# The last MLP's weight blocks: sums taken when the float64 weights are converted, second layer stored split, no GpSimd work in the last stage

## The chip, the cores and the metric

The kernel runs on one core of one Trainium2 chip, as one launch. The metric is device time in microseconds (us). Before the change it is 1503.79 us, the median of 3 runs (1501.11 to 1505.8). The core has five engines with a queue of instructions each: TensorE (PE in the profile; its weight loads are shown as PEld), VectorE (DVE), ScalarE (ACT), GpSimd (POOL) and SyncE (SP). Each works through its queue in order, and waits for another by semaphores. In this kernel SP issues all the large transfers.

## The reference, cut to what matters

An attention, a first MLP over tokens and channels, and then this block, whose last line but one is what the change is about:

```python
def _moe2_ref(x, w_ch1, w_ch2):          # x: 4 x 576 tokens x 512 channels
    X = np.fft.fft(np.fft.fft(x, axis=1), axis=2)
    u = x + np.real(X).astype(np.float32)
    mu = np.mean(u, axis=-1, keepdims=True)
    var = np.mean((u - mu) ** 2, axis=-1, keepdims=True)
    un = (u - mu) / np.sqrt(var + 1e-06)
    ch = np.maximum(un @ w_ch1, 0.0) @ w_ch2     # 512 -> 2048 -> 512
    return (u + ch).astype(np.float32)
```

All weights come as float64. [...]

## The kernel before

**Split products.** A float32 matrix `x` is kept as two parts in the fast matmul format: `hi`, a copy rounded to that format (one ACT instruction), and `lo = x - hi` (one subtraction on DVE or POOL). A product is three matmuls: hi·hi, hi·lo and lo·hi.

**Conversion** (`conv64`). A piece of 512 columns is loaded into a buffer `slot` (three of them), goes through one ACT and five DVE instructions and an addition on POOL (`cadd`), and is stored to DRAM. For the attention's and first MLP's weights (`parts` true) it is split on the way by `chi` (ACT) and `csub` (POOL), and both parts are stored. For the last MLP, 32 pieces of `wm2` are stored unsplit to `wd_d`: for each of 16 hidden blocks `f` of 128, 512 columns of the first layer's weights and 512 of the second's. The conversions run beside the attention.

**The last MLP** (`channel`) has two stages. The first 384 tokens go through plain products (`layer1`, `layer2`), f by f; `first_weights` loads 1024 columns of `wd_d` and splits them (`dwh` on ACT, `dwl` on DVE). The other 1920 tokens are the last stage: three tiles of 640 tokens (`p`), and for each eight pairs of hidden blocks (`q`), so 24 pairs (p, q). The first layer of a pair is a product of 2 x 2 blocks, done with seven block products in place of eight, which takes sums and differences of the blocks of both factors:

- `operands(p)` makes the seven parts of the tokens (`TH` on ACT, `TL` and the differences `TA` on DVE), once for each p.
- `factors(p, q)` makes the seven parts of the weights, for every pair anew, thus three times for each q: it loads the four raw blocks (`WR`, 512 KB, into `wraw`), splits the two that are used as they are (`WH` on ACT, `WL` on POOL), makes the four sums in place (`WA`, POOL), splits these (`WH`, `WL`), all into `wc` (two buffers), and loads and splits the second layer's weights (`VR`, 512 KB; `VH` on ACT, `VL` on POOL) into `v` (three buffers).
- `pair(p, q)` issues the seven products, `LP` (L1324), six matmuls of 320 columns each, and between them the steps that combine their results: `LE` on ACT (L1334) copies a bank of the accumulator out, `LC` on DVE (L1338) adds another bank to it. A pair needs four results, c11, c22, c21 and c12, and there are three banks: product 3 adds to a bank that the `LC` of c22 must have read. Then `hidden` makes the parts of the ReLU's result: `LH` on ACT (L1343) and `LL` on DVE (L1345), four of each, into `hp` (three buffers).
- `second(p, q)` issues 30 matmuls of 512 columns, `LQ` (L1383), into accumulators `y` and `c`. They run about three pairs behind the products.

So ACT's queue holds `LE`, `WH`, `LH` and `VH` in one line, and DVE's holds `LC` and `LL`.

**What sets the order.** Every step is an `Op` with an engine, a cost and a due time; `Plan.order` runs a list schedule over them and writes the instructions in that order into each engine's queue. `SHIFT` moves the due time of each kind of step. For the kinds named in `SHARED`, the planner adds time when DVE and POOL would work at once. At run time only the queues' order and the semaphores count.

Of the kernel before, what the change touches and what calls it, by code (L numbers as in the profile page):

```python
# [119 lines left out]

SHARED = ("cclamp", "cshift", "csign", "cexp", "cmul", "lo4", "FPUT", "dwl", "yadd", "ql.", "kl.", "q.", "un")


# [1434 lines left out]
```

## Time and profile before

| | us |
|---|---|
| median of 3 runs | 1503.79 |
| the profiled execution, its own time | 1502.83 |
| its span in the profile | 1501.0 |
| PE busy | 1433.9 (96%) |
| PEld busy | 1333.3 (89%) |
| DVE busy | 1048.3 (70%) |
| ACT busy | 760.3 (51%) |
| POOL busy | 860.0 (57%) |

The profiled execution's own time is its span and 1.8 us around it. Busy time of PE includes the modelled end of each matmul, so that it says when PE had work in flight and not that it ran at its rate. The first `LP` product starts at 1128.6 us after the span's start, the last one at 1473.5 us; behind them only `LQ` matmuls and the last additions are left.

### The profile page before, as it was taken

Reading aid. Unit: us, or ns where it says so; the run is one execution under the profiler, and the core shown is the slowest. Engines: PE = TensorE matmul, PEld = TensorE weight load, DVE = VectorE, ACT = ScalarE, POOL = GpSimd, SP = SyncE. Lnnn points to the kernel's source line nnn. Section 1 sums busy time; section 2 is a strip of 40 time slices with the busy share of each in tenths; the row PEclk is TensorE's granted clock in tenths of the full one; section 3 lists DMA queues with packets and bytes.
Section 4 is the critical chain, followed back from the end, with each engine's and each line's share of the span. In section 5 each row is a group of like instructions: output and inputs, shape, how many; then the busy total and the mean of one; then the engine's idle time right before and its main releaser. Section 6 shows DMA issues by size and latency. Waiting matters only on the chain.

```text
span 1501.0 us, 25069 instructions
## 1 busy us (share of the span) xinstructions
PE 1433.9 (96%) x9259; PEld 1333.3 (89%) x9259; DVE 1048.3 (70%) x1927; ACT 760.3 (51%) x1456; POOL 860.0 (57%) x653
## 2 busy tenths in 40 slices
PE   8999999999999999999999999999999998988988
PEld 6777789999999999999999999999988877878877
DVE  7867767878777788787787836757577665675452
ACT  4454577566556654665656545323354543443431
POOL 1444497787776675876677641102228885676651
PEclk8999999999999999999999999999999999999999
DMA  5887767856767676657785538762444222322211
GB/s 147 205 224 198 196 177 209 253 171 192 209 189 238 174 219 190 204 175 184 221 244 173 141 100 228 230 210 60 135 146 128 84 72 84 126 71 71 91 57 50
DMA packets 88661, 242.87 MB, mean 162 GB/s; under 512 B 9363, under 2 KB 18708, under 8 KB 88247
## 3 DMA queue, kind: packets, MB, share of 16 engines
q1 hardware_dynamic: 88538, 241.27, 54.8%
q8 instruction: 73, 1.20, 0.3%
q14 instruction: 50, 0.41, 0.1%
HBM read 164.94 MB, written 36.47 MB: 134 GB/s over the span
## 4 chain that ended last, share of the span: by engine, by line
PE 74%; DVE 8%; POOL 6%; DMA 4%; issue 3%; ACT 3%; SPq 2%; ACTq 0%; POOLq 0%; DVEq 0%
PE av L686 13%; PE bank L586 11%; PE bank L864 9%; PE bank L844 9%; PE s L665 9%; PE bank L1324 6%; DVE hp L1345 5%; PE y L1383 4%; DMA qq<-qx 3%; POOL wraw L1288 3%; POOL wc L1283 2%; PE bank L1174 2%; PE y L1196 2%; PE bank L807 2%; PE c L1020 2%
## 5 line engine op out<-in xcount | busy, mean ns | idle before, releaser
L678 POOL TENSOR_TENSOR pl<-s,ph 128x576 fp32r<-128x576 f32 x192 | 288.5, 1514 | 107.7 <-ACT ph L675 70.7
L592 DVE TENSOR_REDUCE mp<-bank 116x1 f32<-116x384 f32 x480 | 242.7, 551 | 87.9 <-PE bank L586 83.2
L670 ACT ACTIVATE s<-s 128x576 f32<-128x576 f32 (+1 forms) x320 | 189.6, 602 | 156.0 <-PE s L665 110.0
L586 PE MATMUL bank<-kk,qq 128*116 128x384 f32 x960 | 215.8, 349 | 15.3 <-DMA qq<-qx 7.4
L665 PE MATMUL s<-qq,kk 128*128 128x288 f32 (+1 forms) x1152 | 207.4, 303 | 0.6 <-ACT s L670 0.4
L675 ACT ACTIVATE ph<-s 128x576 fp32r<-128x576 f32 (+1 forms) x240 | 151.4, 634 | 106.1 <-PE av L686 104.7
L1324 PE MATMUL bank<-tt,wc 128*128 128x320 f32 x1008 | 168.3, 318 | 37.4 <-DVE e L1338 32.4
L1324 PEld LDWEIGHTS bank<-tt,wc 128*128 128x128 f32 x1008 | 156.6, 194 | 48.3 <-DVE e L1338 36.8
L586 PEld LDWEIGHTS bank<-kk,qq 128*116 128x116 f32 x960 | 161.7, 182 | 27.5 <-issue 10.1
L665 PEld LDWEIGHTS s<-qq,kk 128*128 128x128 f32 (+1 forms) x1152 | 177.8, 192 | 6.7 <-ACT s L670 1.4
L1283 POOL TENSOR_TENSOR wc<-wraw,wc 128x512 fp32r<-128x512 f32 (+2 forms) x72 | 111.0, 1557 | 115.3 <-ACT wc L1281 104.8
L844 PE MATMUL bank<-ut,w 128*128 128x320 f32 (+1 forms) x1152 | 176.2, 297 | 0.0
L1345 DVE SCALAR_TENSOR_TENSOR hp<-e,hp 128x320 fp32r<-128x320 f32 x96 | 115.4, 1248 | 69.5 <-ACT hp L1343 69.3
L864 PE MATMUL bank<-h,w 128*128 128x320 f32 (+1 forms) x1152 | 162.9, 296 | 0.1
L844 PEld LDWEIGHTS bank<-ut,w 128*128 128x128 f32 x1152 | 159.6, 190 | 0.0
L864 PEld LDWEIGHTS bank<-h,w 128*128 128x128 f32 x1152 | 156.4, 189 | 0.5 <-DVE h L768 0.4
L362 POOL TENSOR_TENSOR slot<-slot 128x512 f32<-128x512 f32 (+2 forms) x62 | 82.4, 1330 | 98.9 <-DVE slot L359 72.4
L686 PE MATMUL av<-pl,vh 128*65 128x288 f32 x432 | 127.0, 294 | 1.1 <-POOL pl L678 1.1
L686 PE MATMUL av<-ph,vh 128*65 128x288 f32 x432 | 127.7, 296 | 0.3 <-ACT xtr L691 0.3
L686 PE MATMUL av<-ph,vl 128*65 128x288 f32 x432 | 126.9, 294 | 0.0
L873 DVE TENSOR_TENSOR yt<-bank,yt 128x256 f32<-128x256 f32 (+1 forms) x192 | 85.7, 454 | 43.0 <-PE bank L864 40.7
L1383 PE MATMUL y<-v,hp 128*128 128x512 f32 x432 | 111.3, 396 | 0.0
(149 smaller groups left out, 2507.3 us busy)
## 6 DMA issues: line engine op xcount, KB each, us to landing
w<-wb_d SPq DMA_DIRECT2D x96, 512.0 KB, 4.3
slot<-in_wm_dram SPq DMA_DIRECT2D x56, 512.0 KB, 5.1
wraw<-wd_d SPq DMA_DIRECT2D x40, 512.0 KB, 3.8
kk<-kx SPq DMA_DIRECT2D x30, 576.0 KB, 5.0
wb_d<-slot SPq DMA_DIRECT2D x24, 512.0 KB, 3.7
vraw<-wd_d SPq DMA_DIRECT2D x24, 512.0 KB, 3.7
v<-in_v_dram SPq DMA_DIRECT2D x32, 292.5 KB, 4.2
qx<-in_qT_dram SPq DMA_DIRECT2D x15, 576.0 KB, 6.2
```

The lines of the kernel that those rows point to most:

```text
L586: nc.tensor.matmul(bank.t[:QM, :KW], qq.t[:r, t, q0:q0 + QM], kk.t[:r, t, c * KW:(c + 1) * KW], start=(t == 0), stop=(t == 1))
L592: tops.append(add("mr" + own_place, "V", t_dve(KW), dd, lambda bank=bank, j=j, c=c: nc.vector.tensor_reduce(out=mp.t[:QM, j, c:c + 1], in_ ...
L665: nc.tensor.matmul(ps.t[:, j, :HQ], kk.t[:r, t, (c0 + j) * 128:(c0 + j + 1) * 128], qq.t[:r, t, qs], start=(t == 0), stop=(t == 1))
L670: a = add(f"exp{own_place}{gr}", "A", t_act(n * HQ), due + 0.1, lambda ps=ps, s=s, n=n: nc.scalar.activation(out=s.t[:, :n], in_=ps.t[:, : ...
L675: h = add(f"hi{gr}", "A", t_act(n * HQ), due + 0.25, lambda ph=ph, s=s, n=n: nc.scalar.activation(out=ph.t[:, :n], in_=s.t[:, :n], func=AF ...
L678: a = add(f"lo{gr}", e, t(n * HQ), due + 0.4, lambda s=s, ph=ph, pl=pl, eng=eng, n=n: eng.tensor_tensor(out=pl.t[:, :n], in0=s.t[:, :n], i ...
L686: nc.tensor.matmul(po.t, vx.t[:, c0 + j], x.t[:, j], start=first and k == 0, stop=last and k == len(pairs) - 1)
L844: mms.append(lambda ps, k=len(mms), kk=kk, wi=wi, xi=xi, t0=t0, n=n: nc.tensor.matmul(ps[:, :n], view("p (s k n) -> p s k n", s=2, k=4)[:, ...
L864: mms.append(lambda ps, k=len(mms), x=x, wi=wi, hi=hi, cc=cc, t0=t0, n=n: nc.tensor.matmul(ps[:, :n], ww[x][2]("p (s n) -> p s n", s=2)[:, ...
L1324: nc.tensor.matmul(ps.t[:, :PH], w.t[:, wi, k, 128 * kk:128 * kk + 128], x.t[:, xi, kk], start=(first and m == 0), stop=(last and m == 5), ...
L1345: return [a, add("LL", "V", t_dve(PH), base(p, q) + SL * (slots[i] + 1) / 17, lambda: nc.vector.scalar_tensor_tensor(out=h.t[:, k, 1, cols ...
L1383: nc.tensor.matmul(y.t, h.t[:, k, hi, j * 128:(j + 1) * 128], v.t[:, wi, k], start=(q == 0 and k == 0 and n == 0), stop=(q == 7 and k == 1 ...
```

## The change

The four sums are made where the weights are converted, and stored beside the raw blocks, so that the last stage loads all seven (`w1_d`, 7 x 256 columns, 896 KB for a pair). `conv64` gets an argument `sums`: four POOL instructions of 128 columns in place (`cs`) behind `cadd`, and one more store. The host lays `wm2` out so that one piece of 512 columns holds one half of a pair's four blocks. The second layer's pieces are now split at the conversion (`parts` true) and stored as `w2_d` (1024 KB for a pair). In the last stage `WH` and `WL` become one instruction each of 1792 columns, `WL` on DVE; `WA`, `VH` and `VL` are gone; `VR` loads straight into `v`; and `wraw` has one buffer where there were two. In `first_weights` the second layer's half is loaded split (`dwv`), and `dwh` and `dwl` have 512 columns. Nearly every value of `SHIFT` is another one, and `SHARED` has four more kinds.

```diff
-    "cvld": 22.77, "cabs": 91.18, "cclamp": 306.7, "cshift": 206.5, "csign": 124.94, "cexp": 45.41, "cmul":
...
+    "cvld": 18.95, "cabs": 336.18, "cclamp": 653.39, "cshift": 93.62, "csign": 86.53, "cexp": 67.74, "cmul":
...
-SHARED = ("cclamp", "cshift", "csign", "cexp", "cmul", "lo4", "FPUT", "dwl", "yadd", "ql.", "kl.", "q.", "un")
+SHARED = ("TL", "TA", "LL", "WL", "cclamp", "cshift", "csign", "cexp", "cmul", "lo4", "FPUT", "dwl", "yadd", "ql.", "kl.", "q.", "un")
...
-    wd_d = dram.tile([F2, 128, 1024], F32, name="wd_d")
+    w1_d = dram.tile([F2 // 2, 128, 8, 2, 128], F32, name="w1_d")
+    w2_d = dram.tile([F2, 128, 2, 512], F32, name="w2_d")
...
+            if sums is not None:
+                done = a
+                for k, (x, y, op) in enumerate(((-4, -1, ALU.add), (0, -3, ALU.subtract), (-3, -4, ALU.subtract), (-2, 1, ALU.subtract))):
...
+                    done = add("cs", "P", t_pool(128), due, lambda k=k, x=x, y=y, op=op, quarter=quarter: nc.gpsimd.tensor_tensor(
+                        out=quarter(k), in0=quarter(x), in1=quarter(y), op=op), [done], uses=[w])
+                r.append(add("cvst", "SP", t_dma(512 * n), due, lambda: nc.sync.dma_start(
+                    out=sums, in_=f32(hi()).rearrange("p (s n) -> p s n", n=128)), [done], uses=[w]))
...
-        for f in range(F2):
-            for o in range(0, 1024, 512):
-                store((2, f), conv64(
-                    90.0 + f * 1.0, wm2[f][:, o:o + 512], [(wd_d[f][:, o:o + 512], same)], False))
+        for q in range(F2 // 2):
+            for k in range(2):
+                store((2, q), conv64(90.0 + 2 * q, wm2[q][:, 512 * k:512 * k + 512], [(w1_d[q][:, :4, k], blocks)], False, w1_d[q][:, 4:, k]))
+            for k in range(2):
+                store((3, 2 * q + k), conv64(
+                    91.0 + 2 * q, wm2[q][:, 1024 + 512 * k:1536 + 512 * k], [(w2_d[2 * q + k], same)], True))
...
-        vraw_r = late(1, "vraw", "mp", [128, 2, C])
+        wraw_r = late(1, "raw7", "mp", [128, 1792])
...
+                o = add("WR", "SP", t_dma(512 * 1792), d - 1.5, lambda: nc.sync.dma_start(
+                    out=raw.t.rearrange("p (i k n) -> p i k n", k=2, n=128), in_=w1_d[q][:, 1:]), ready, new=[raw])
...
-                w_ops = piece(0, 0, 512, 0, [o])
-                w_ops += piece(1, 768, 1024, 512, [o])
-                s1 = sums(0, 3, 2, 3, ALU.add, w_ops)
-                s3 = sums(1, 2, 0, 2, ALU.subtract, [s1])
-                s2 = sums(2, 0, 3, 0, ALU.subtract, [s3])
-                s4 = sums(3, 1, 1, 0, ALU.subtract, [s2])
-                w_ops += piece(5, 0, 1024, 768, [s4])
...
-                a = add("VH", "A", t_act(1024), d + 1.2, lambda: nc.scalar.activation(
-                    out=v.t[:, 0], in_=vraw.t, func=AF.Copy), [o] + late_w, new=[v], uses=[vraw])
...
+                a = add("WH", "A", t_act(1792), d, lambda: nc.scalar.activation(
+                    out=of(0), in_=raw.t, func=AF.Copy), [o], new=[w], uses=[raw])
+                b = add("WL", "V", t_dve(1792), d, lambda: nc.vector.tensor_tensor(
+                    out=of(1), in0=raw.t, in1=f32(of(0)), op=ALU.subtract), [a], uses=[raw, w])
+                o = add("VR", "SP", t_dma(512 * 2048), d, lambda: nc.sync.dma_start(
+                    out=f32(v.t), in_=w2_d[2 * q:2 * q + 2].rearrange("f p s n -> p s f n")), ready + late_w, new=[v])
+                return w, [a, b], v, [o]
```

On DVE, near the end of the program, this is the order for three pairs before (L1338 is `LC`, L1345 is `LL`):

```order
L1338 TENSOR_TENSOR e<-bank,e 128x320 x4
L1345 SCALAR_TENSOR_TENSOR hp<-e,hp 128x320 x4
L1338 TENSOR_TENSOR e<-bank,e 128x320 x4
L1345 SCALAR_TENSOR_TENSOR hp<-e,hp 128x320 x4
L1338 TENSOR_TENSOR e<-bank,e 128x320 x3
```

and now (L1337 is `LC`, L1344 is `LL`, L1301 is the new `WL`):

```order
L1337 TENSOR_TENSOR e<-bank,e 128x320 x4
L1301 TENSOR_TENSOR wc<-raw_16625,wc 128x1792
L1344 SCALAR_TENSOR_TENSOR hp<-e,hp 128x320 x4
L1337 TENSOR_TENSOR e<-bank,e 128x320 x4
L1344 SCALAR_TENSOR_TENSOR hp<-e,hp 128x320 x4
L1337 TENSOR_TENSOR e<-bank,e 128x320 x3
```

One long instruction came between a pair's additions and its `LL` block; the rest of the line is as it was. A group of four `LC` holds c22, c21 and c12 of one pair and c11 of the next.

On ACT at the same place, one pair before (L1334 is `LE`, L1281 `WH`, L1343 `LH`, L1303 `VH`):

```order
L1334 ACTIVATE e<-bank 128x320
L1281 ACTIVATE wc<-wraw 128x512
L1281 ACTIVATE wc<-wraw 128x256
L1334 ACTIVATE e<-bank 128x320 x2
L1281 ACTIVATE wc<-wraw 128x1024
L1343 ACTIVATE hp<-e 128x320 x4
```

and now (L1333 is `LE`, L1299 `WH`, L1342 `LH`):

```order
L1342 ACTIVATE hp<-e 128x320 x4
L1333 ACTIVATE e<-bank 128x320 x3
L1299 ACTIVATE wc<-raw_16625 128x1792
L1342 ACTIVATE hp<-e 128x320 x4
L1333 ACTIVATE e<-bank 128x320 x3
```

Before, the `WH` of 1024 columns, which splits the sums, stood in front of the four `LH`; now the one `WH` stands there.

On POOL, the last pairs before (L1283 is `WL`, L1288 `WA`, L1305 `VL`):

```order
L1283 TENSOR_TENSOR wc<-wraw,wc 128x1024
L1305 TENSOR_TENSOR v_16604<-vraw,v_16604 128x1024
L1283 TENSOR_TENSOR wc<-wraw,wc 128x512
L1283 TENSOR_TENSOR wc<-wraw,wc 128x256
L1288 TENSOR_TENSOR wraw<-wraw 128x256 x4
```

and now a piece near the end of the attention (L694 is the attention's `pl`, L363 `cadd`, L368 `csub`, L377 the new `cs`):

```order
L694 TENSOR_TENSOR pl<-s,ph 128x576 x2
L377 TENSOR_TENSOR slot<-slot 128x128
L694 TENSOR_TENSOR pl<-s,ph 128x576 x2
L363 TENSOR_TENSOR slot<-slot 128x512
L377 TENSOR_TENSOR slot<-slot 128x128
L694 TENSOR_TENSOR pl<-s,ph 128x576
L377 TENSOR_TENSOR slot<-slot 128x128
```

POOL's work for the last MLP now stands between the attention's instructions. Of the 64 `cs` and 16 new `csub`, 16 and 4 stand behind the attention's last `pl`, beside the Fourier transform, together with 7 `cadd`; the last instruction of POOL's queue is one of the transform's additions.

## Rows read from the trace of the kernel before

**Rows 1.** Stretches: us; busy (count) of PE, PEld, DVE, ACT, POOL; clock, DMA, GB/s.

```profile
40.00:865.00 825.00, 808.14 (x5552) 764.05 (x5551) 638.62 (x1228) 490.07 (x921) 551.30 (x399) 1.00 0.70 199
865.00:1043.30 178.30, 175.50 (x1318) 171.33 (x1317) 108.15 (x257) 64.30 (x141) 34.12 (x38) 1.00 0.57 174
1128.60:1473.80 345.20, 307.79 (x1671) 275.06 (x1670) 207.07 (x263) 147.89 (x288) 240.46 (x184) 0.98 0.26 85
```

**Rows 2.** Groups on PE by line, 1128.6 to 1473.8: busy, mean ns, idle before.

```profile
L1324 PE MATMUL bank<-tt,wc 128*128 128x320 f32 x1008 | 168.3, 318 | 37.4 <-DVE e L1338 32.4 <-ACT e L1334 5.0
L1383 PE MATMUL y<-v,hp 128*128 128x512 f32 x367 | 96.0, 397 | 0.0
L1383 PE MATMUL c<-v,hp 128*128 128x512 f32 x252 | 61.9, 390 | 0.0
L1139 PE MATMUL bank<-ident,un 128*128 128x128 f32 x40 | 5.7, 285 | 0.0
```

**Rows 3.** Chain that ended last, 1400 to 1501: start, us, what.

```profile
1432.42 3.51 PE bank L1324 x24
...
1438.54 4.92 DVE hp L1345 x3
...
1476.51 2.72 PE c L1383 x12
```

**Rows 4.** Timeline of one pair: start, us, engine, line, what, idle before it.

```profile
1423.57 5.66 DVE L1345 SCALAR_TENSOR_TENSOR hp<-e,hp 128x320 fp32r<-128x320 f32 x4 [4.65 <-ACT hp L1343]
...
1429.16 1.07 DVE L1338 TENSOR_TENSOR e<-bank,e 128x320 f32<-128x320 f32 x2
...
1429.69 2.03 PE L1324 MATMUL bank<-tt,wc 128*128 128x320 f32 x12 [1.71 <-DVE e L1338]
...
1432.25 3.67 PE L1324 MATMUL bank<-tt,wc 128*128 128x320 f32 x24
...
1436.88 1.06 ACT L1281 ACTIVATE wc<-wraw 128x1024 fp32r<-128x1024 f32 x1 [2.24 <-POOL wraw L1288]
...
1438.03 1.19 ACT L1343 ACTIVATE hp<-e 128x320 fp32r<-128x320 f32 x3
```

**Rows 5.** Lines L1345 and L1338: count, ns min/median/max.

```profile
L1345 DVE SCALAR_TENSOR_TENSOR hp<-e,hp x96: 469/814/2771, 1132.2 to 1478.3; 128x320 fp32r<-128x320 f32 x96
...
L1338 DVE TENSOR_TENSOR e<-bank,e x96: 465/492/494, 1131.1 to 1473.8; 128x320 f32<-128x320 f32 x96
```

**Rows 6.** Groups on POOL by line, 970 to 1501.

```profile
L1283 POOL TENSOR_TENSOR wc<-wraw,wc 128x512 fp32r<-128x512 f32 (+2 forms) x72 | 111.0, 1557 | 115.3 <-ACT wc L1281 104.8 <-PE y L1383 9.4 <-PE bank L1324 1.2
L1288 POOL TENSOR_TENSOR wraw<-wraw 128x256 f32<-128x256 f32 x96 | 82.8, 862 | 7.5
...
L1305 POOL TENSOR_TENSOR v<-vraw,v 128x1024 fp32r<-128x1024 f32 x24 | 60.6, 2527 | 23.1 <-ACT v L1303 23.1
```

**Rows 7.** Groups by form, whole span, that price the new instructions.

```profile
L367 POOL TENSOR_TENSOR slot<-slot 128x512 fp32r<-128x512 f32 x27 | 36.4, 1351 | 17.1 <-ACT slot L365 17.0
...
L1281 ACT ACTIVATE wc<-wraw 128x1024 fp32r<-128x1024 f32 x24 | 25.5, 1061 | 49.0 <-POOL wraw L1288 49.0
...
L1112 DVE TENSOR_TENSOR w<-wraw,w 128x1024 fp32r<-128x1024 f32 x16 | 19.5, 1218 | 9.8 <-ACT w L1110 9.7
```

**Rows 8.** SP's issues between 1286 and 1288, then the stretch of 1 us that ends them.

```profile
1286.41 0.36 SPq L1300 DMA_DIRECT2D vraw<-wd_d  x1
1286.82 0.46 SPq L1273 DMA_DIRECT2D wraw<-wd_d  x1
1287.33 0.46 SPq L1121 DMA_DIRECT2D u<-u_d  x1
...
1295.00:1296.00 1.00, 1.00 (x6) 0.83 (x5) 0.00 (x0) 0.82 (x1) 0.15 (x1) 1.00 0.14 45
```

**Rows 9.** Stretches of 10 us: the two of lowest clock in the stage.

```profile
1160.00:1170.00 10.00, 7.19 (x35) 6.41 (x34) 9.43 (x17) 6.49 (x16) 9.69 (x8) 0.83 0.17 54
...
1350.00:1360.00 10.00, 8.24 (x34) 7.69 (x35) 6.22 (x10) 3.25 (x6) 5.45 (x6) 0.66 0.23 73
```

More of the change, by code (lines that the diff above doesn't have):

```diff
@@ L76 @@
-    -220.37, "LP": -176.18, "LE": 274.63, "LC": -205.45, "LH": -55, "LL": 114.93, "LQ": 315.6,
+    "cvld": 18.95, "cabs": 336.18, "cclamp": 653.39, "cshift": 93.62, "csign": 86.53, "cexp": 67.74, "cmul":
+    24.33, "cadd": 136.67, "chi": 229.31, "csub": 137.36, "cvst": 12.38, "cs": 193.21, "warm.": -10.38, "l.":
+    -170.47, "q.": 3.29, "qh.": 173.09, "ql.": -56.56, "kh.": 73.63, "kl.": -86.48, "M.": -726.75, "mr.": 22.61,
+    "zh.": -56.2, "mr2.": -99.98, "zl.": -207.73, "mT.": 12.63, "mrow.": -142.63, "vld": -151.06, "S.": -27.39,
[6 rows of a table added]
@@ L77 @@
+    -401.58, "TH": 382.16, "TL": -581.56, "TA": -170.63, "WR": 111.46, "WH": -199.81, "WL": -528.64, "VR":
+    -831.72, "LP": -551.07, "LE": 609.89, "LC": -780.38, "LH": 25.74, "LL": 290.03, "LQ": 824.98,
 }
@@ L325, in tile_attention_moe_fnet, with conv64 @@
         converted = []
-        def conv64(due, src, outs, parts):
+        def conv64(due, src, outs, parts, sums=None):
             w = Buf(cvw)
@@ L1271, in factors @@
                 d = base(p, q) - 2.2
-                raw, w = Buf(craw_r), Buf(wc_r)
-                o = add("WR", "SP", t_dma(512 * 1024), d - 1.5, lambda: nc.sync.dma_start(
-                    out=raw.t.rearrange("p (f n) -> p f n", f=2),
-                    in_=wd_d[2 * q:2 * q + 2].rearrange("f p n -> p f n")[:, :, :C]), [more] + stores[2, 2 * q] + stores[2, 2 * q + 1], new=[raw])
+                raw, w, v = Buf(wraw_r), Buf(wc_r), Buf(v2_r)
+                ready = [more] + stores[2, q] + stores[3, 2 * q] + stores[3, 2 * q + 1]
@@ L1287, in sums @@
-                def sums(n, dst, x, y, op, deps):
-                    return add("WA", "P", t_pool(256), d + 0.3 + 0.05 * n, lambda: nc.gpsimd.tensor_tensor(
-                        out=raw.t[:, 256 * dst:256 * dst + 256], in0=raw.t[:, 256 * x:256 * x + 256],
-                        in1=raw.t[:, 256 * y:256 * y + 256], op=op), deps, uses=[raw])
-                w_ops = piece(0, 0, 512, 0, [o])
-                w_ops += piece(1, 768, 1024, 512, [o])
-                s1 = sums(0, 3, 2, 3, ALU.add, w_ops)
@@ L1295, in factors @@
-                s3 = sums(1, 2, 0, 2, ALU.subtract, [s1])
-                s2 = sums(2, 0, 3, 0, ALU.subtract, [s3])
-                s4 = sums(3, 1, 1, 0, ALU.subtract, [s2])
-                w_ops += piece(5, 0, 1024, 768, [s4])
-                vraw, v = Buf(vraw_r), Buf(v2_r)
-                o = add("VR", "SP", t_dma(512 * 1024), d, lambda: nc.sync.dma_start(
-                    out=vraw.t, in_=wd_d[2 * q:2 * q + 2].rearrange("f p n -> p f n")[:, :, C:]),
-                    [more] + stores[2, 2 * q] + stores[2, 2 * q + 1], new=[vraw])
@@ L1317, in product @@
                     x, x_ops = t[i]
[L1318 removed]
+                    k = {1: 0, 2: 1, 3: 6, 4: 2, 5: 3, 6: 4, 7: 5}[i]
                     def products():
@@ L1537 @@
     a_m1 = units(inputs["moe_w_ch1"], inputs["moe_w_ch2"], F1)
-    a_m2 = units(inputs["moe2_w_ch1"], inputs["moe2_w_ch2"], F2)
+    m = units(inputs["moe2_w_ch1"], inputs["moe2_w_ch2"], F2).reshape(F2 // 2, 2, 128, 8, 128)
+    a_m2 = _np.empty((F2 // 2, 128, 16, 128), m.dtype)
+    for k in range(2):
+        for n, (f, b) in enumerate(((1, k), (0, k), (0, 2 + k), (1, 2 + k))):
+            a_m2[:, :, 4 * k + n] = m[:, f, :, b]
+        a_m2[:, :, 8 + 4 * k:12 + 4 * k] = m[:, k, :, 4:]
+    a_m2 = a_m2.reshape(F2 // 2, 128, 2048)
     names = ["kT", "qT", "v", "wt1", "wt2", "wm1", "wm2", "cs", "ss", "cd", "sd", "nyq"]
```

42 lines of the change are left out of this document (18 added, 24 removed), and 12 rows, old and new, of the table SHIFT.

## Prediction

> **What bounds the kernel now.** I first read busy time by stretch. PE is busy 97.9% of the attention's stretch and 98.4% of the Fourier transform's, but 307.8 of 345.2 us where the seven-product scheme runs, which leaves 37.4 us idle there [rows 1]. Next I read who ended that idle time: all 37.4 us stand before `LP` (L1324), 32.4 until an `LC` on DVE and 5.0 until an `LE` on ACT [rows 2].
>
> Busy time flatters PE, since a matmul's modelled end covers small gaps. In the chain 24 `LP` take 3.51 us and 12 `LQ` 2.72 us [rows 3], so 0.146 and 0.227 us each at full rate. The stretch holds 1008 `LP`, 619 `LQ` and some 44 small ones [rows 2]: 147.4 + 140.3 + about 5 (the 40 transposes are busy 5.7 at most) = 293 us. So **345 - 293 = 52 us** is the most that the stage can give back: 37.4 of idle time and some 15 of gaps inside busy groups and of slow clock. The clock granted is 0.98 on average there and 1.00 in the stretches ahead [rows 1].
>
> Then one pair in order of time. `LL` blocks start at 1423.57 and 1438.54 [rows 4, 3], a period of 14.97 us, against 42 x 0.146 + 30 x 0.227 = 12.94 us of work on PE: 2.0 us lost. Four `LL` take 5.66 us; the `LC` behind them starts as they end, at 1429.16, and PE, which has waited 1.71 us, goes on at 1429.69 [rows 4]. Why is the block long and late? Long: an `LL` takes 0.47 us at least but 2.77 at most, with half of them above 0.81, while `LC`, of the same 320 columns, never leaves 0.465 to 0.494 [rows 5]. `LL` reads two tiles of the core's buffer, `LC` one and a bank of the accumulator; so what stretches `LL` is what POOL, busy 240 of 345 us [rows 1], does in the buffer. Late: `LL` waited 4.65 us for ACT's `LH`, and these stand behind the `WH` of 1024 columns, which waited 2.24 us for POOL's sums [rows 4]. POOL enters the path twice.
>
> **The change in the last stage.** It removes all 192 POOL instructions of the stage: 111.0 + 82.8 + 60.6 = 254 us of POOL [rows 6]. Without them, 96 `LL` at 0.485 us take 47 us. It adds 24 `WL` of 1792 columns to DVE. The nearest row is a subtraction of 1024 columns in the same form, 1.22 us [rows 7], which makes at most 1792/1024 x 1.22 = 2.1 us (at least 1.22); I take 2.1, since a duration here grows nearly with the columns, and so 50 us on DVE. ACT's `WH` is by the same step at most 1.86 us from 1.06 [rows 7]. ACT loses the waits for POOL's sums.
>
> Now the new period. T is when the 24 `LP` of a pair end. PE then has 27 `LQ` and 6 `LP`, 6.12 + 0.88 = 7.0 us, and after that product 3, which needs c22. Before: the 24 ended at 1435.93 [rows 3], `LH` came at T + 2.1, `LL` at T + 2.6 and ended 5.66 later, at T + 8.3, c22 at T + 8.8 [rows 4]; 8.8 - 7.0 gives the stall of 1.7 again. After, in the queues' order: the last `LE` ends near T + 0.6, `WH` at T + 2.5, `WL` at T + 4.75 (0.2 between engines), the four `LL` (their `LH` are done by then, at 0.4 each) at T + 6.7, c22 at T + 7.25, and PE sees it at T + 7.45. **A stall of 0.45 us** is left in place of 2.0, so 24 x 0.45 = 11 us of the 52 stay. What is late next is the same c22, held by `WH` and `WL` in one piece. I leave 4 us more for the three changes of p and the first pairs, where the seven token parts are made on DVE as well. So the stage gives 52 - 11 - 4 = 37 us. The bounds: 52, if the four ends overlap better than my line, and 52 - 30 = 22 if `WL` or `WH` comes 0.8 us later than I have it in each pair.
>
> The clock is part of this. [...] It falls where PE has waited: 1160 to 1170 at 0.83, PE idle for 2.8 us of it, and 1350 to 1360 at 0.66, idle for 1.8 [rows 9]. [...] If the waits left at the changes of p kept the clock down as often as now, the sum below would end at 1475 (rival 5). [...]
>
> **The transfers.** Per pair, `WR` grows from 512 to 896 KB and `VR` from 512 to 1024. `wraw` has one buffer, so a `WR` is issued only when the `WL` before has read it, about T + 4.8, and `VR` when an `LQ` group has freed `v`, about T + 2.7. Both must have landed at T + 12.94 + 0.6, thus within 10.8 us of `VR`. Three loads of 512, 512 and 1280 KB issued from 1286.41 on were through shortly after 1295 [rows 8]: 2304 KB in 8.9 us. 1920 KB then take 7.4, and the load is hidden with 3 us to spare.
>
> **The conversions.** POOL gets 64 `cs` and 16 `csub`. A `csub` is 1.35 us [rows 7]; a `cs` of 128 columns is at most the 0.86 of 256 columns [rows 6] and, halved, 0.43. So 64 x 0.43 + 16 x 1.35 = 49 us; 12 of it and 7 `cadd` (9 us) stand behind the attention, so the attention's 825 us get 28 more on POOL's 551, and the transform's 178 us get 21 on 34 [rows 1]. PE idles 16.9 us in the attention's stretch [rows 1]. If that grew as POOL's idle time shrinks (273.7 to 246), it would be 1.9 us more. The bounds are 0, since POOL is idle a third of that time, and 28, if all of it lay on the path. I take 2, nearest to the rows. ACT's 16 `chi` and 16 more stores and 16 more loads by SP lie beside it; the transfers there are busy 0.70 of the time and grow by about 8 MB of some 164. The 49 us might also hold DVE up there as POOL does in the last stage: then DVE's 638.6 of 825 us become 688 at most, and PE's 16.9 us of idle time, scaled as DVE's idle time shrinks (186 to 137), grow by 6, so that the sum below would end at 1472 (rival 6). [...] `first_weights` gets shorter on ACT and DVE; I count nothing: PE is at 98% in the stretch that holds its first part, so that 3 us are the most it could give. The new `SHIFT` values reorder the attention's queues; with PE at 98% I give that nothing, with 6 us either way in the range.
>
> **Sum.** 1502.83 (the profiled execution: span 1501.0 and 1.8 around it) - 37 + 2 = 1467.8. The median of the runs is 1.0 above that execution, hence **1468 to 1469; I say 1468.**
>
> **Rivals.** (1) *DVE takes POOL's place*: `WL` in one piece before the `LL` block, and `WH` before the `LH`, so that c22 comes 0.8 us later still. For it: both stand in one line with no gap in the order; DVE's load per pair, 1.95 + 1.94 + 2.1 and its share of the token parts, stays where it was. Against: my line already has them in full length. 24 x 1.25 = 30 us stay: 1503.8 - 52 + 30 + 4 + 2 = 1488. (2) *The wait is not POOL's*: `LL` gets short, but `LH` is late for another reason, so c22 stays. For it: `LL` waited 4.65 us for ACT, more than its stretch costs. Against: ACT itself waited for POOL. Time 1502 to 1506. (3) *The transfers bind, slower*: with one `wraw`, a load that takes more than 10.8 us from `VR` on stalls every pair, and from 12.6 us on the period is above the old one. At 15 us the period would be 12.94 + 4.2 = 17.1, that is 24 x 2.2 = 53 us more than before: 1557; at 13 us some 1510. For it: the bytes nearly double, and the loads wait for DVE. Against: rows 8's 2304 KB in 8.9 us. (4) *All of the 52 come back and the new order helps in the attention*: 1452 or less. (5) *The slow clock stays* (above): 1475; for it, the changes of p keep their chain of token parts; against, the waits that go are most of those the clock fell behind. (6) *The conversions hold DVE* (above): 1472; for it, `LL` shows the stretch; against, a late DVE reaches PE only where PE waits for it.
>
> **Chances.** My sum 0.50, between 1455 and 1481, which holds rivals 5 and 6 too, 0.08 and 0.12; rival 1 0.15 (1482 to 1498); rival 2 0.05; rival 3, or the conversions costing more than the stage gives, 0.06; rival 4 0.04. The range that leaves out the last three and the upper part of rival 1 is 1454 to 1491. A measurement of this kernel tells about 0.3% from no change, 4.5 us: faster 0.50 + 0.20 + 0.15 + 0.04 = 0.89, same 0.05, slower 0.06.
>
> **What would show it.** In the changed profile POOL is idle from the last addition of the transform on; `LL` is 0.47 to 0.50 us throughout; `WL` near 2 us, `WH` near 1.8; the idle time before `LP` falls from 37 to some 10 us; the period near 13.4; clock 1.00 in the stage; POOL about 50 us more before it. The prediction is wrong if `LP` waits for `WL` or for a load, if `LL` still has a wide spread without POOL, or if PE's idle time in the attention grows by more than 10 us.

## The result, and the profile after

The changed kernel takes **1449.7 us** (median of 4 runs, 1447.7 to 1452.4), the kernel before 1502.5 in the same session: a ratio of 0.965, 95% interval 0.962 to 0.967. The direction was forecast; the time lies 18 us below the 1468 and 4 below the range. The profiled execution took 1447.66, its span is 1445.9.

The same three stretches as in [rows 1], the last one with the new stage's ends (columns: us; busy and count of PE, PEld, DVE, ACT, POOL; clock, DMA share, GB/s):

```profile
40.00:865.00 825.00, 815.66 (x5627) 774.42 (x5626) 602.62 (x1200) 497.26 (x935) 578.60 (x452) 1.00 0.71 202
865.00:1043.30 178.30, 173.10 (x1291) 168.50 (x1290) 129.01 (x301) 65.30 (x148) 60.78 (x69) 0.99 0.73 216
1113.50:1417.60 304.10, 302.34 (x1702) 273.81 (x1701) 175.57 (x297) 126.27 (x227) 0.00 (x0) 1.00 0.49 167
```

The last stage is 304 us instead of 345, PE idles 1.8 us in it instead of 37.4, POOL does nothing, and the clock is 1.00. But PE is also busier by 7.5 us in the attention's 825 us, where the forecast saw no gain, and the stage begins 15 us earlier. About half of these 15 us is not gain: 37 more of the plain stage's matmuls run inside the last stage now and not ahead of it (27 of L1215, where 4 did before, and 14 of L1193).

Groups on PE in the stage, answering to [rows 2] (busy, mean ns, idle before):

```profile
L1323 PE MATMUL bank<-tt,wc 128*128 128x320 f32 x1008 | 157.7, 310 | 1.8 <-ACT e L1333 1.1 <-DVE tt L1268 0.5 <-DVE e L1337 0.2
L1382 PE MATMUL y<-v,hp 128*128 128x512 f32 x361 | 90.7, 392 | 0.0
L1382 PE MATMUL c<-v,hp 128*128 128x512 f32 x252 | 63.8, 392 | 0.0
L1215 PE MATMUL y<-w,h 128*128 128x512 f32 x27 | 6.9, 392 | 0.0
L1158 PE MATMUL bank<-ident,un 128*128 128x128 f32 x40 | 5.7, 272 | 0.0
L1193 PE MATMUL bank<-ut,w 128*128 128x384 f32 x14 | 2.8, 336 | 0.0
```

At the full rates of the prediction, 0.146 us an `LP` and 0.227 a matmul of 512 columns, this is 147.2 for the `LP`, 640 x 0.227 = 145.3 for the 512-column ones, and some 7 for the 54 small ones (at most 8.5 by their busy time): 299.5 in all. So about **4.6 us are lost in the stage, where 52 were.**

`LL` and `LC` as in [rows 5], then the new `WH` and `WL` (ns min/median/max):

```profile
L1344 DVE SCALAR_TENSOR_TENSOR hp<-e,hp x96: 480/486/494, 1124.1 to 1423.4; 128x320 fp32r<-128x320 f32 x96
...
L1337 DVE TENSOR_TENSOR e<-bank,e x96: 481/492/493, 1115.6 to 1417.6; 128x320 f32<-128x320 f32 x96
...
L1299 ACT ACTIVATE wc<-raw x24: 1684/1690/1705, 1106.8 to 1396.0; 128x1792 fp32r<-128x1792 f32 x24
L1301 DVE TENSOR_TENSOR wc<-raw,wc x24: 2004/2018/2027, 1108.5 to 1397.7; 128x1792 fp32r<-128x1792 f32 x24
```

One pair in order of time, answering to [rows 4] (start, us, engine, line, what, idle before):

```profile
1393.68 3.68 PE L1323 MATMUL bank<-tt,wc 128*128 128x320 f32 x24
...
1395.97 1.69 ACT L1299 ACTIVATE wc<-raw 128x1792 fp32r<-128x1792 f32 x1
...
1397.70 2.03 DVE L1301 TENSOR_TENSOR wc<-raw,wc 128x1792 fp32r<-128x1792 f32 x1 [2.37 <-ACT wc L1299]
...
1400.15 1.55 ACT L1342 ACTIVATE hp<-e 128x320 fp32r<-128x320 f32 x4 [2.48 <-PE y L1382]
1400.65 1.70 DVE L1344 SCALAR_TENSOR_TENSOR hp<-e,hp 128x320 fp32r<-128x320 f32 x4 [0.93 <-ACT hp L1342]
1401.61 0.42 ACT L1333 ACTIVATE e<-bank 128x320 f32<-128x320 f32 x1
1402.27 0.48 DVE L1337 TENSOR_TENSOR e<-bank,e 128x320 f32<-128x320 f32 x1
...
1402.67 1.62 PE L1323 MATMUL bank<-tt,wc 128*128 128x320 f32 x10
```

T, the end of the 24 `LP`, is 1397.36. `WH` started 1.4 us ahead of it. The four `LL` take 1.70 us instead of 5.66; the `LC` behind them starts at T + 4.9, and PE goes on without a wait. What these `LL` waited for was not `WL`, which ended at T + 2.4, but `LH`; and `LH` waited 2.48 us for `LQ` matmuls, which free the `hp` buffer that it writes.

### The profile page after: what moved, and what is told of

It reads as the page before. It is cut to its first block, busy times and chain, and to the rows that moved or that the text cites. A ratio compares the mean times of both kernels' runs of the same rounds, so it can differ in the third digit from the quotient of the medians.

```text
span 1445.9 us, 24938 instructions
## 1 busy us (share of the span) xinstructions
PE 1420.8 (98%) x9259; PEld 1328.3 (92%) x9259; DVE 981.0 (68%) x1951; ACT 734.8 (51%) x1400; POOL 655.9 (45%) x541
## 4 chain that ended last, share of the span: by engine, by line
PE 92%; DMA 4%; DVE 2%; ACT 1%; SPq 1%; issue 0%; DVEq 0%; ACTq 0%
PE av L702 15%; PE bank L602 11%; PE s L681 10%; PE bank L1323 10%; PE bank L860 10%; PE bank L880 10%; PE y L1382 7%; PE c L1382 5%; PE bank L1193 2%; PE y L1215 2%; PE bank L823 2%; PE c L1036 2%; PE bank L795 2%; PE c L1055 1%; PE bank L830 1%; DMA slot<-in_wm_dram 1%
## 5 line engine op out<-in xcount | busy, mean ns | idle before, releaser
L694 POOL TENSOR_TENSOR pl<-s,ph 128x576 fp32r<-128x576 f32 x192 | 289.0, 1516 | 99.1 <-ACT ph L691 67.1
L1323 PE MATMUL bank<-tt,wc 128*128 128x320 f32 x1008 | 157.7, 310 | 1.8 <-ACT e L1333 1.1
L1323 PEld LDWEIGHTS bank<-tt,wc 128*128 128x128 f32 x1008 | 151.6, 188 | 8.0 <-ACT e L1333 2.8
L363 POOL TENSOR_TENSOR slot<-slot 128x512 f32<-128x512 f32 (+2 forms) x62 | 80.4, 1297 | 109.8 <-DVE slot L360 91.5
L1382 PE MATMUL y<-v,hp 128*128 128x512 f32 x432 | 107.3, 392 | 0.0
L1337 DVE TENSOR_TENSOR e<-bank,e 128x320 f32<-128x320 f32 x96 | 47.1, 491 | 79.3 <-PE bank L1323 56.3
L1382 PEld LDWEIGHTS y<-v,hp 128*128 128x128 f32 x432 | 79.7, 188 | 15.1
```

The source lines that it names most:

```text
L694: a = add(f"lo{gr}", e, t(n * HQ), due + 0.4, lambda s=s, ph=ph, pl=pl, eng=eng, n=n: eng.tensor_tensor(out=pl.t[:, :n], in0=s.t[:, :n], i ...
L1323: nc.tensor.matmul(ps.t[:, :PH], w.t[:, wi, k, 128 * kk:128 * kk + 128], x.t[:, xi, kk], start=(first and m == 0), stop=(last and m == 5), ...
L1382: nc.tensor.matmul(y.t, h.t[:, k, hi, j * 128:(j + 1) * 128], v.t[:, wi, k], start=(q == 0 and k == 0 and n == 0), stop=(q == 7 and k == 1 ...
```

## The experiments

Every run stands beside runs of the kernel before on the same chip (medians of 1499.6 to 1502.5 us); the other columns are of the profiled execution. "Lost" is the stage's length less PE's busy time in it; the stage reaches from the first `LP` to the last. "Attention" is PE's idle time from 40 to 885 us.

| run | us | attention | stage starts | stage | lost | LL median, longest (us) |
|---|---|---|---|---|---|---|
| before | 1502 | 16.9 | 1128.6 | 345.2 | 37.4 | 0.81, 2.77 |
| after | 1449.7 | 9.3 | 1113.5 | 304.1 | 1.8 | 0.49, 0.49 |
| after, GpSimd reads added | 1494.2 | 8.1 | 1118.7 | 345.6 | 31.2 | 1.00, 2.72 |
| the same, planned | 1478.6 | 8.8 | 1113.5 | 335.3 | 19.0 | 0.92, 2.70 |
| after, GpSimd memsets added | 1449.8 | 8.7 | 1116.4 | 303.9 | 1.8 | 0.49, 0.49 |
| before, GpSimd memsets instead | 1457.6 | 16.0 | 1127.9 | 300.7 | 3.9 | 0.49, 0.51 |
| before, new marks | 1462.5 | 16.8 | 1130.3 | 310.7 | 5.9 | 1.03, 2.69 |
| before, new order | 1471.6 | 11.9 | 1141.0 | 305.3 | 4.9 | 0.84, 2.69 |
| before, new early values | 1506.7 | 12.6 | 1136.1 | 342.4 | 33.3 | 0.52, 2.69 |
| before, marks and early values | 1465.8 | 12.9 | 1135.2 | 300.3 | 3.7 | 1.02, 2.70 |
| after, old early values | 1517.0 | 18.9 | 1179.2 | 305.4 | 9.2 | 0.48, 0.49 |
| after, old attention values | 1499.1 | 34.5 | 1169.1 | 302.4 | 1.1 | 0.48, 0.49 |
| after, `WL` twice | 1475.5 | 10.2 | 1117.1 | 328.6 | 19.3 | 0.48, 0.50 |
| before, conversions added | 1514.7 | 22.8 | 1142.9 | 342.9 | 32.2 | 0.54, 2.75 |
| the same, arithmetic on 8 columns | 1517.7 | 22.2 | 1140.9 | 343.5 | 35.1 | 0.69, 2.77 |
| the same, stores on 8 columns too | 1517.3 | 25.9 | 1147.0 | 341.6 | 35.0 | 0.83, 2.69 |
| after, conversions out of the plan | 1466.6 | 11.0 | 1135.3 | 303.5 | 1.6 | 0.48, 0.49 |
| after, conversions on 8 columns | 1448.5 | 8.8 | 1113.9 | 304.0 | 1.8 | 0.49, 0.50 |

Five of these runs have the changed kernel's plan on every engine (after, reads added, memsets added, `WL` twice, conversions on 8 columns). Their attention idles 8.1 to 10.2 us, and their last stage starts between 1113.5 and 1118.7: so much varies with the same order.

### Is it GpSimd's reading?

**GpSimd's load, given back to the changed kernel.** In `factors`, behind `WL`:

```diff
+                    if 8 * p + q > 2:
+                        x = craw_r.make()
+                        for n in (512, 256, 256, 256, 256, 256, 1024, 1024):
+                            nc.gpsimd.tensor_tensor(out=x[:, :n], in0=f32(of(0))[:, :n], in1=f32(of(1))[:, :n], op=ALU.subtract)
```

> The changed kernel, with eight GpSimd subtractions put behind each WL from the fourth weight pair on (512, four of 256 and a fifth of 256, two of 1024 columns, reading the pair's split weights from SBUF and writing a buffer that nobody reads): GpSimd's load of the last stage of before without anybody waiting for its results. This is extra work. Theory A (GpSimd's reads stretch VectorE's two-operand instructions, and that stretch is what the last stage of before paid): mean LL 1.0 to 1.4 us instead of 0.486, four LL in a block about 5 us instead of 1.7, the stage 330 to 345 us instead of 304, the time 1475 to 1492 us. Theory B (the new order of the last stage hides the stretch, as it did for the old work under the new order, whose stage took 305 us with mean LL 1.05): LL stretched just as much, the stage 304 to 312, the time 1449 to 1459 us.

1494.2 us, +44. The two halves of the stage, then its `LL` (busy, mean ns, idle before), then who ended PE's waits over the span (us, times, longest):

```profile
1118.70:1320.00 201.30, 190.50 (x1054) 170.03 (x1053) 150.16 (x195) 82.48 (x149) 121.68 (x89) 0.99 0.47 162
1320.00:1464.30 144.30, 123.88 (x649) 109.06 (x648) 99.67 (x102) 43.67 (x79) 109.53 (x80) 0.95 0.36 126
```

```profile
L1350 DVE SCALAR_TENSOR_TENSOR hp<-e,hp 128x320 fp32r<-128x320 f32 x92 | 90.7, 1013 | 25.8 <-ACT hp L1348 24.7
```

```profile
PE bank L1329 <- DVE e L1343: 20.7, 12, 5.5
PE bank L1329 <- DVE wc L1302: 5.1, 8, 1.5
PE bank L1329 <- ACT e L1339: 4.7, 4, 2.2
```

Nobody waits for GpSimd's results here, and most of the old loss is back (31.2 of 37.4 us): theory A, with a time 2 us above its range. Some of it is new, though: PE waits 5.1 us for `WL`, which the old last stage had on GpSimd. The halves tell more. In VectorE's order of the changed kernel `LC` (C) and `LL` (L) alternate in the first pairs, as in CLCLCCLL, and stand in blocks, CCCCWLLLL, in the last ones. The stage lost 10.8 of 201 us in the first part and 20.4 of 144 in the second.

**The same time on GpSimd, without reading.**

```diff
+                        nc.gpsimd.tensor_tensor(out=x[:, :8], in0=f32(of(0))[:, :8], in1=f32(of(1))[:, :8], op=ALU.subtract)
+                        for _ in range(10):
+                            nc.gpsimd.memset(x, 0.0)
```

> The changed kernel, with ten GpSimd memsets of 128x1024 (and one subtraction of 8 columns ahead of them, so that they start with each pair) behind each WL from the fourth pair on: GpSimd is about as busy in the last stage as in before, but hardly reads. Extra work. If GpSimd's reading is what stretches LL: LL stays near 0.49 us, the stage 304, the time 1448 to 1453 us. If any GpSimd access to SBUF does it: LL 0.8 to 1.4 us and the time as with the GpSimd subtractions.

1449.8 us, no difference from the changed kernel. GpSimd and `LL` in the stage, by form:

```profile
L1307 POOL MEMSET wraw<- 128x1024 f32 x210 | 201.1, 957 | 12.1
```

```profile
L1351 DVE SCALAR_TENSOR_TENSOR hp<-e,hp 128x320 fp32r<-128x320 f32 x92 | 42.3, 487 | 26.4 <-ACT hp L1349 25.4
```

207 us of GpSimd that writes leave `LL` at 0.487.

**The kernel before, with its order and its waits, but without the reading.** Each GpSimd step of the last stage:

```diff
+            def fill(y, x0, x1, op):
+                nc.gpsimd.tensor_tensor(out=y[:, :8], in0=x0[:, :8], in1=x1[:, :8], op=op)
+                for _ in range(2):
+                    nc.gpsimd.memset(f32(y), 0.5)
```

> The kernel before with its plan and order untouched; in the last stage every GpSimd subtraction or addition is replaced by one on 8 columns, which keeps its waits, and two memsets of its output, so that GpSimd stays about as long (some 180 of its 240 us) but hardly reads; the low parts and sums of the last MLP's weights are wrong. If reading alone was the harm: LL from 1.25 to about 0.49 us, the stage from 345 to 305-312, with the old blocks of four LL and with GpSimd's results still waited for, 1460 to 1470 us. If GpSimd's lateness (its results waited for by ScalarE and TensorE) was part of the stage's loss: the stage 325 to 345, 1480 to 1500 us.

1457.6 us, a ratio of 0.970 (0.967 to 0.974). The stage and its `LP`:

```profile
1127.90:1428.60 300.70, 296.76 (x1671) 268.51 (x1670) 123.39 (x262) 144.71 (x288) 223.32 (x550) 1.00 0.29 99
```

```profile
L1330 PE MATMUL bank<-tt,wc 128*128 128x320 f32 x1008 | 159.2, 310 | 3.9 <-DVE e L1344 2.3 <-ACT e L1340 1.4
```

GpSimd is still busy 223 of 301 us (240 of 345 before), in the same places of the same order, and ACT still waits for its sums, 64.9 us over the whole span where it waited 49.0 ([rows 7]):

```profile
L1286 ACT ACTIVATE wc<-wraw 128x512 fp32r<-128x512 f32 (+2 forms) x72 | 47.8, 698 | 99.0 <-POOL wraw L1273 64.9
```

Yet the 37 us of idle time fall to 3.9. So in this order the reading was the harm, and the lateness of GpSimd's results cost next to nothing by itself.

### Or the order?

**The whole new order on the old work.** `SHIFT` and `SHARED` of after in the kernel before (`WA`, `VL` at the value of `WL`; `VH` at that of `WH`):

```diff
-    "cvld": 22.77, "cabs": 91.18, ...
+    "cvld": 18.95, "cabs": 336.18, ...
-SHARED = ("cclamp", "cshift", ...
+SHARED = ("TL", "TA", "LL", "WL", "cclamp", "cshift", ...
```

> The kernel before, with the due times (SHIFT) and the SHARED kinds of the change; no work is moved. Theory A (POOL's work in the last stage held PE, and the new order counts for little): POOL still stretches LL and still holds ACT, so 1490 to 1505 us, with 25 us or more of PE idle time before LP. Theory B (the retuned order is what gained, in the last stage too): below 1475 us and less than 15 us idle before LP.

1471.6 us, a ratio of 0.980 (0.978 to 0.983), with all of GpSimd's work in place. Theory A, that the order counts little, fell. The stage:

```profile
1141.00:1446.30 305.30, 300.38 (x1683) 271.43 (x1682) 190.18 (x268) 151.43 (x293) 247.80 (x184) 0.99 0.29 98
```

**The four marks alone.** One line of the kernel before, whose values of `SHIFT` all stay (`WL` is GpSimd's here, so that its mark does nothing):

```diff
-SHARED = ("cclamp", "cshift", "csign", ...
+SHARED = ("TL", "TA", "LL", "WL", "cclamp", "cshift", "csign", ...
```

> [...] On VectorE the pattern of a pair turns from CCCCLLLL (four LC, then four LL) into interleaved ones such as CLCLCCLL. Theory A (what the last stage of before paid is LC waiting behind a block of stretched LL): last stage 345 to about 305-312 us with GpSimd's 240 us of work still in it and mean LL still near 1 us, start of the stage as before (1128.6), time 1458 to 1470 us. Theory B (the gain of the new order needs its whole table): 1485 to 1502 us.

1462.5 us, a ratio of 0.974 (0.972 to 0.976): 40 us from a planner that adds time to `LL` where GpSimd works at once. VectorE's order over the last pairs, before and with the marks:

```
before  CCCCLLLLCCCCLLLLCCCCLLLLCCCLLLL
marks   CCLCLLCLCLCCLLCLCLCCLLCLCLCCLL
```

Its `LL`, and `LP` in the stage:

```profile
L1344 DVE SCALAR_TENSOR_TENSOR hp<-e,hp x96: 479/1026/2693, 1140.7 to 1442.0; 128x320 fp32r<-128x320 f32 x96
```

```profile
L1323 PE MATMUL bank<-tt,wc 128*128 128x320 f32 x1008 | 160.7, 313 | 5.9 <-ACT e L1333 3.2 <-POOL wc L1282 2.6
```

`LL` is stretched as before (its median even longer), and in the stage PE no longer waits for DVE at all. The stretched `LL` harm where the `LC` of the next pair stands behind four of them (37.4 us lost before, 5.9 here). The marks moved a second wait as well: ACT's `WH` wait 8.0 us for GpSimd's sums in this stage, where they waited 46.6 before. This run alone does not tell the two apart. The added reads do, since nobody waits for GpSimd there and the loss is back, and so do the memsets, which keep that wait without the loss.

**The added reads again, planned.** The eight subtractions are recorded as steps on engine "P", so that the planner sees them:

```diff
+                    for i, n in enumerate((512, 256, 256, 256, 256, 256, 1024, 1024)):
+                        prev = add("XR", "P", t_pool(n), d, lambda n=n, i=i: load(n, i == 0), [prev], uses=[w])
```

> The same eight GpSimd subtractions behind each WL from the fourth pair on as in the run with GpSimd's reads (1494 us), but recorded as operations of the planner, which then sees GpSimd busy and interleaves LC and LL on VectorE (the last pairs go from CCCWLLLL to CCLCLWCLL and the like). If what costs is LC waiting behind a block of stretched LL: LL stretched to 0.9 us or more as before, but TensorE loses under 15 us in the stage, 1453 to 1468 us. If the stretch itself costs, whatever the order: 1485 to 1500 us.

1478.6 us: between the two. The order gave back 15.5 of the 44 us. What is left in the stage:

```profile
L1333 PE MATMUL bank<-tt,wc 128*128 128x320 f32 x1008 | 169.6, 318 | 19.0 <-DVE e L1347 7.8 <-DVE wc L1301 5.0 <-DVE tt L1268 3.8
```

```profile
L1301 DVE TENSOR_TENSOR wc<-raw,wc 128x1792 fp32r<-128x1792 f32 x23 | 59.2, 2572 | 7.6 <-ACT wc L1299 7.6
```

Here VectorE has `WL` too, 1792 columns that read two tiles, 2.57 us on average and not 2.02. So with `WL` on VectorE the order hides only part of GpSimd's reading; with `WL` on GpSimd (the marks on the old work) it hid nearly all. That the stretched `WL` is the reason was not tested by itself.

### How much room is in the new stage?

```diff
+                    for _ in range(2):
+                        nc.vector.tensor_tensor(out=of(1), in0=raw.t, in1=f32(of(0)), op=ALU.subtract)
```

> The kernel of the change, with each WL of 1792 columns on DVE run twice (the second run writes the same values). The prediction's chain of one pair had WL on the path with no slack, and a stall of 0.45 us left: each of the 24 pairs then loses 2.0 us more, 1495 to 1500. The timeline of the change shows DVE idle for 0.93 us between WL and LL and c22 ready about 0.7 us ahead of product 3: then a pair loses some 0.4 us, 1455 to 1465.

1475.5 us, between both: 2.02 us more on VectorE for each of 24 pairs cost 25.8 / 24 = 1.07 each. On average the pair had some 0.95 us of room, about the 0.93 for which VectorE sat idle behind `WL` in the pair shown above. Most of PE's 19.3 us of waiting is for the doubled `WL` itself, by a product that needs its weights, and only 2.7 us is for an `LC`:

```profile
PE bank L1326 <- DVE wc L1303: 12.2, 15, 1.3
```

### What happens ahead of the last stage?

**The new early values on the old work** (`SHIFT` of after up to the Fourier stage, no marks), and then with the marks:

```diff
-    "cvld": 22.77, "cabs": 91.18, ... "bs": -282.17, "pm": 85.41, "yadd": 610.91, ...
+    "cvld": 18.95, "cabs": 336.18, ... "bs": 95, "pm": -99.14, "yadd": 14.48, ...
```

> The kernel before with the SHIFT values of after for everything up to the Fourier stage (conversions, attention, first MoE, Fourier); values for the channel stage and the last MLP, and SHARED, as before. On VectorE the last stage keeps its pattern CCCCLLLL. If the changed kernel's earlier start of the last stage (1113.5 instead of 1128.6) comes from its early order: the last stage starts at 1112 to 1120 and takes 340 to 350, time 1485 to 1493 us. If the early order gains nothing without the new work: start 1126 to 1142 (1141.0 with the whole new table), time 1498 to 1515 us.

> The kernel before with both moves of the table at once: the four marks in SHARED and the SHIFT values of after for everything up to the Fourier stage. If the two are independent: the marks' 39.6 us less, the early values' 4.6 more, 1465 to 1469 us, the stage of the last MLP with under 10 us lost (345 to about 310). If the early values of after are worth the 7.6 us of TensorE's idle time in attention that the changed kernel saves, and only the last stage of the old work spoilt it: 1452 to 1458 us.

1506.7 and 1465.8 us. The attention saves 4 us of idle time (12.6 and 12.9 for 16.9), but the stretch behind it, to the first `LP`, idles 10.3 and 9.0 us instead of 2.8, so that nothing is left. The first of them, 40 to 885 us and on to the stage:

```profile
40.00:885.00 845.00, 832.45 (x5738) 788.42 (x5737) 643.93 (x1240) 502.89 (x948) 561.96 (x407) 1.00 0.69 197
885.00:1136.10 251.10, 240.77 (x1611) 227.30 (x1610) 158.10 (x347) 87.34 (x181) 42.62 (x53) 0.98 0.52 157
```

**The old early values on the new work** (everything ahead of `first_weights`; `cs` at the old value of `cadd`), and the old values of the attention and first MLP alone:

```diff
-    "l.": -170.47, "q.": 3.29, "qh.": 173.09, ... "open": -24.3, "sqrt": -82.81,
+    "l.": -318.21, "q.": 4.64, "qh.": 130.94, ... "open": -492.22, "sqrt": 18.95,
```

> The kernel of the change, with the due times of before for everything ahead of the last MLP (conversions, attention, first MLP, Fourier transform) and those of the change from first_weights on. Theory A: the last stage keeps its gain, and what the profiles show elsewhere, some 7 us, goes: 1454 to 1460 us, last stage 302 to 308 us long. Theory B: above 1465. If the order ahead counts for nothing at all: 1448 to 1452.

> The changed kernel with the SHIFT values of before for the attention and the first MLP alone (conversions, Fourier, channel and last MLP as after). On VectorE the last stage turns to blocks CCCCWLLLL from its fourth pair on. If the new values of the attention are what saves TensorE 7.6 us there: idle time from 40 to 885 us at 15 to 18 us again instead of 9.3, time 1455 to 1462 us. If the attention's order is worth nothing: 1447 to 1453. In both cases, if blocks of four LL do no harm without GpSimd's reading: LL 0.486 us and under 6 us lost in the stage; if blocks are bad in themselves, 20 us or more lost there and 1470 us or more.

1517.0 and 1499.1 us: all of the gain, and in the first run more, is lost ahead of the stage, whose own loss stays at 9.2 and 1.1. In the first, there is one wait of 20.5 us for a normalisation, and a granted clock of 0.63 on average in the 40 us around it:

```profile
PE bank L1157 <- DVE un L1150: 20.5, 1, 20.5
```

```profile
1140.00:1180.00 40.00, 14.70 (x79) 11.30 (x77) 18.28 (x47) 9.55 (x22) 4.40 (x6) 0.63 0.56 197
```

In the second, PE idles 34.5 us in the attention, where 15 to 18 was the most expected. Both tables are mixtures that were fitted to neither kernel, so neither gives a price for the old order as such. But the second shows something else: its last stage stands mostly in blocks, CCCCWLLLL, from the fourth pair on, and loses 1.1 us. Blocks do no harm where `LL` takes 0.48:

```profile
1169.10:1471.50 302.40, 301.33 (x1699) 273.48 (x1698) 172.75 (x295) 123.64 (x227) 0.00 (x0) 1.00 0.49 166
```

**The conversions, added to the kernel before** (work and stores that nobody uses), then with their arithmetic on 8 columns, then with their stores on 8 columns as well:

```diff
+                        done = add("cs", "P", t_pool(128), due, ...
+                    done = add("chi", "A", t_act(n), due, ...
+                    done = add("csub", "P", t_pool(n), due, ...
+                r.append(add("cvst", "SP", t_dma(512 * n), due, ...
```

> The kernel before, with the conversion work of the change added and its results stored but not used: 64 more instructions of 128 columns and 16 more of 512 on POOL, 16 more copies on ACT, 8 MB more stored. Its price alone. The prediction's term: 2 us, so 1502 to 1507. If POOL holds DVE there as it does in the last stage: 6 us or more, 1508 to 1515. If it all hides: 1500 to 1504.

> The kernel before with the added conversions in its plan (the run that took 1514.7 us), whose added arithmetic is executed on 8 columns only; the added stores stay. If the 12.7 us came from the shifted plan and the stores: 1511 to 1516 us. If they came from the arithmetic's time on GpSimd and ScalarE: 1501 to 1506 us.

> The kernel before with the added conversions in its plan, whose arithmetic (as in the run at 1517.7 us) and now also whose 32 added stores move 8 columns only. If the stores' bytes made the old kernel slower: 1500 to 1506 us. If it is the plan, in which everything behind an added operation comes in another place: 1510 to 1518 us.

1514.7, 1517.7 and 1517.3 us: 13, 16 and 18 us more than the kernel before beside them (1.009, interval 1.007 to 1.011, for the first), so the loss stays when first the arithmetic and then the bytes are gone. 40 to 885 us of the first and of the last:

```profile
40.00:885.00 845.00, 822.16 (x5625) 773.50 (x5624) 640.06 (x1222) 500.02 (x940) 594.85 (x468) 1.00 0.70 202
```

```profile
40.00:885.00 845.00, 819.12 (x5600) 770.12 (x5598) 634.59 (x1217) 492.14 (x937) 560.98 (x467) 1.00 0.68 193
```

PE idles 22.8 and 25.9 us where it idled 16.9, whether POOL is busy 595 us or 561. What is left is the plan, in which the new steps push others to other places, and the issuing of 32 more stores by SP, which remains in all three and is not told apart from it.

**The conversions, taken from the changed kernel**: out of its plan, and then with the plan kept and the arithmetic on 8 columns.

```diff
-                for k, (x, y, op) in enumerate(((-4, -1, ALU.add), (0, -3, ALU.subtract), ...
+                for k, (x, y, op) in enumerate(((-4, -1, ALU.add),) * 0):
...
-                        return f32(lo() if i < 0 else hi())[:, 128 * (i % 4):128 * (i % 4) + 128]
+                        return f32(lo() if i < 0 else hi())[:, 128 * (i % 4):128 * (i % 4) + 8]
```

> The changed kernel without the added arithmetic of the conversions: the four cs of a piece and the second layer's chi and csub are left out, and the stores write the converted value in their place, with the same bytes; the last MLP computes with wrong weights. If the additions cost in the new order what they cost in the old one (12.7 us): 1435 to 1441 us. If the new order hides them, as the prediction put them at 2 us: 1445 to 1451 us.

> The changed kernel with its plan, and so the order on every engine, untouched; but the added arithmetic of the conversions (cs, and the second layer's chi and csub) is executed on 8 columns instead of 128 and 512, so its work is left out and the last MLP's weights are wrong. Where the run with these operations taken out of the plan (1466.6 us, 17 slower) was slower because the plan came out another way, this one shows what the arithmetic itself costs: if it is hidden, 1446 to 1451 us; if it costs what the old order paid for it (12.7 us), 1435 to 1441 us.

1466.6 us with less work: 17 us *slower*, which neither side expected, since the plan came out another way (the stage starts at 1135.3, not 1113.5). 1448.5 with the plan kept:

```profile
40.00:885.00 845.00, 836.22 (x5785) 794.55 (x5784) 615.87 (x1221) 504.28 (x957) 569.57 (x465) 1.00 0.70 200
```

So the arithmetic costs 1.2 us at most, inside the spread of the runs.

## Why the prediction was right, and where it was wrong

**What bound the kernel: right.** The 52 us of the last stage, and what stretched `LL`. With GpSimd's reading gone and the old plan kept, 37.4 us of idle time become 3.9; with reading put back, 1.8 become 31.2. On average `LL`, with two tiles of the buffer to read, takes 0.487 us beside 207 us of memsets and 1.01 beside 231 us of subtractions; `LC`, with one tile and a bank, takes 0.490 and 0.486.

**"POOL enters the path twice": half wrong.** The second entrance, sums that come late and hold up `WH` and `LH`, was not a cost of its own. With the memsets in GpSimd's place the waits were kept and the loss was gone.

**The prices of `WL` and `WH`: right.** 2.02 us (forecast 2.1) and 1.69 (at most 1.86). `cs` took 0.50 (forecast 0.43). `LL` came out at 0.486 (0.485).

**The stall of 0.45 us: the first step that failed.** I had "the last `LE` ends near T + 0.6, `WH` at T + 2.5". In the queue as it ran, `WH` stands ahead of that `LE` and of the `LH`: it began at T - 1.4, and `WL` was done at T + 2.4, before `LH` let the `LL` start. (That `LE` itself ran behind the `LH` and ended at T + 4.7.) So the `LC` of c22 ended at T + 5.4, where my line had T + 7.25, and by the prediction's count PE has other work until T + 7.0. No row shows the 0.2 us that this line puts between engines: it is the planner's allowance (`lag`), and in the pair above `WL` starts 0.04 us behind the end of `WH`. The period is 12.99 us (`LL` blocks at 1400.65 and 1413.64), the pure work 12.94; forecast 13.4. The stage gave back 52 - 4.6 = 47.4 us, not 37: the terms of 11 for the stall and 4 for the changes of p were 10.4 too much. With 0.95 us of room shown by the doubled `WL`, rival 1 was a matter of one microsecond a pair.

**"With PE at 98% I give that nothing": the second step that failed.** The new order saves PE 7.5 us of idle time in the attention (16.9 to 9.3), and the range had 6 either way. Sum: 1502.83 - 47.4 - 7.5 = 1447.9, within 0.3 of the profiled execution's own time; so the two terms (10.4, and 7.5 where I had a loss of 2) account for the 20 us. That it closes so well is in part luck: from 885 us to the first `LP` PE idles 5.2 us where it idled 2.8, and over all that lies ahead of the stage its idle time falls by 6.1 us. A run shows the two terms apart: without the reading, but with the old plan, the kernel takes 1457.6 us and its attention still idles 16.0; the 7.9 us from there to 1449.7 are about the 6.7 us of idle time that its attention has more. Which part of the new plan saves them is open, since the new early values alone saved 4 us on the old work and lost them again behind the attention. How wrong the *size* was is seen in the runs with other tables: the last stage began anywhere between 1113.5 and 1179.2. PE at 98% bounds what an order can gain; it does not bound what an order can lose.

**The conversions at +2: right for the work, and beside the point.** Their arithmetic costs 1.2 us or nothing; rival 6 (6 us) fell. The same steps cost the old table 13 to 18 us as entries of its plan, with or without their arithmetic and bytes.

**The rivals.** Rival 2, that the wait was not POOL's, fell: `LL` got short and the waits went with it. Rival 3 fell too: the loads of 896 and 1024 KB land in 5.8 and 5.5 us at the median, and PE waits for none in the stage. (Its 12.6 us should have been 12.8: 10.8 and the 2.0 us between 12.94 and 14.97.) Rival 5 fell: its 1475 is the 1468 and 7 us, 2% of the stage's 345 by the mean clock of 0.98 in [rows 1], and the clock is now 1.00 there. What came was rival 4, with 47.4 of the 52 us and a gain from order in the attention; I gave it 0.04.

**What I did not see.** The loss needed two things at once: a stretched `LL`, and an order in which `LC` stands behind four of them. Either cure works without the other: no reading with the old blocks (1457.6), or interleaving with all the reading (1462.5). The change has the first throughout and the second only in its first pairs; standing mostly in blocks (the old attention values) its stage loses no more, 1.1 us, so in the stage it is the missing reading that pays. With `WL` on VectorE the reading costs even a planner that sees it 29 us (1478.6), and 44 one that does not. Whether the old work, with a table fitted to it throughout, would reach 1449.7 was not tried; with one line changed (1462.5) it is 12.8 us away, and idles 4.1 us more in the last stage (5.9 for 1.8) and 7.5 more in the attention (16.8 for 9.3).
